# Constant 64-column products in TensorE's planned idle time of the first passes, and a new table of order shifts

## The chip, the cores and the metric

The kernel runs on one core of one Trainium2 chip. The metric is device time in microseconds (us), the median of several executions. Beside each kernel stands one profiled execution, whose span (first to last instruction) and own time are given with it. A difference of less than 0.3% is about what a measurement of this kernel can't tell from none.

## The reference

Attention with a block-causal mask, then two feed-forward layers, all in fp32:

```python
# q, k, v: (4, 8, 576, 64); w_in: (512, 2048), w_out: (2048, 512), twice
scores = q @ k.T / 8;  mask: key block (64 wide) <= query block
x = softmax(scores) @ v                      # -> 2304 tokens x 512
h = x @ w_in;  x = (h * tanh(softplus(h))) @ w_out       # layer 0
h = max(x @ w_in2, 0);  out = (h * h) @ w_out2           # layer 1
```

## The kernel before

The 2304 tokens are cut into six chunks of 384 tokens (CH1). Chunks 0 and 1 hold the first 192 tokens of two batches each (attention_lo, fp32 products), chunks 2 to 5 the last 384 tokens of one batch each (attention_hi, products of fp16 pairs). Each chunk goes through layer 0 and layer 1, so there are twelve passes over it (PASSES); a pass has 16 blocks f, each of which makes 12 products of 384 columns into a bank hp (line 1129), an activation on ScalarE (1135), and 12 products into the four banks acc (1195). Pass 0 is done in fp32 instead (lines 1149 and 1164). The weights arrive as words that VectorE and ScalarE first turn into fp32 (decode, lines 992 to 998) and then into fp16 pairs (split, lines 1008 to 1016 and parts, 966 to 967 and 678); the pairs go to DRAM and come back for later passes. This decoding, the attention of chunks 0 to 3 and the first passes share the first 230 us.

Nothing in the order of the program is left to a run-time scheduler. The class Sched (line 161) holds a list of tasks with an engine, a cost and dependencies each; forward (336) simulates the engines, takes at each step the ready task with the lowest rank, and gives it a start; the instructions are then issued in the order of those starts (1412 to 1417), on every engine and on the DMA queue (SP). The rank is a due time less a lead, and the lead takes a hand-held number of ns from the table SHIFT for each group of tasks: the attention of a chunk (att, av), the decoding of a weight unit (decode, weigh, split), the scaling of a chunk (scale, norm). A change of SHIFT so changes the order on all engines.

Sched.clock (227) models TensorE's clock: work counts at half speed in a stretch of time that follows a stretch with little work. Sched.fill (239) counts how many constant products (ones times ones, 128 columns, bf16) fit ahead of a TensorE task into the time in which TensorE is planned idle, and half of them are issued there (line 1416). It is called only while the pair of banks called spare is still free, that is until the first task of the rings ab and s1 on TensorE; afterwards no such products are issued.

spare is one tile of two PSUM banks of 512 fp32 columns. Columns 0 to 447 of both hold attention scores and their products: the ring ab takes both banks at once (attention_hi), the ring s1 alternately the one and the other (attention_lo). Columns 448 to 511 of bank 0 hold results of one to eight columns: sc (split, line 1009), qm (scale_of, 741), vm (halves, 693), sx (chunk_scale, 1070). Columns 448 to 511 of bank 1 are used by nothing. The planner holds these column ranges for separate resources. The waits between engines are put in by the framework when the program is built, from what each instruction reads and writes.

Of the kernel before, what the change touches and what calls it, by code (L numbers as in the profile page):

```python
# [56 lines left out]
def seg_len(tiles):  # L57
# [25 lines left out]


SHIFT = {
    ('att', 0, 0): 2800, ('att', 0, 1): 5100, ('att', 0, 2): -400, ('att', 0, 3): -4900,
    ('att', 0, 4): -400, ('att', 0, 5): 200, ('att', 0, 6): -800, ('att', 0, 7): -19200,
    ('att', 1, 0): 18800, ('att', 1, 1): 20600, ('att', 1, 2): 6300, ('att', 1, 3): -900,
    ('att', 1, 4): 29600, ('att', 1, 5): -29900, ('att', 1, 6): -33600, ('att', 1, 7): -28200,
    ('att', 2, 0): 200, ('att', 2, 1): -500, ('att', 2, 2): -900, ('att', 2, 3): 1000,  # L90
    ('att', 3, 0): -600, ('att', 3, 1): -500, ('att', 3, 2): 15300, ('att', 3, 3): 12900,
    ('att', 4, 0): -5700, ('att', 4, 1): 16600, ('att', 4, 2): 63500, ('att', 4, 3): 46400,
    ('att', 5, 0): -41600, ('att', 5, 1): 37300, ('att', 5, 2): 6700, ('att', 5, 3): 71800,
# [8 lines left out]
    ('decode', 0, 0, 0): -12000, ('decode', 0, 0, 1): 500, ('decode', 0, 0, 2): -22800, ('decode', 0, 0, 3): 21300,  # L102
    ('decode', 0, 0, 4): -19000, ('decode', 0, 0, 5): 5800, ('decode', 0, 1, 0): 21900, ('decode', 0, 1, 2): 119000,
    ('decode', 0, 1, 3): -17400, ('decode', 0, 1, 4): -11600, ('decode', 0, 1, 5): 100, ('decode', 0, 1, 6): 2900,
    ('decode', 1, 0, 0): -2900, ('decode', 1, 0, 1): -5700, ('decode', 1, 0, 2): 2500, ('decode', 1, 0, 3): 6300,
    ('decode', 1, 0, 4): 6800, ('decode', 1, 0, 5): 300, ('decode', 1, 0, 6): -600, ('decode', 1, 0, 7): -500,
    ('decode', 1, 1, 0): 1200, ('decode', 1, 1, 1): -14800, ('decode', 1, 1, 2): 17100, ('decode', 1, 1, 3): -20100,
    ('decode', 1, 1, 4): -1200, ('decode', 1, 1, 5): -5000, ('decode', 1, 1, 6): -14700, ('decode', 1, 1, 7): 50100,
    ('norm', 0, 1): -4700, ('norm', 0, 2): 4300, ('norm', 0, 3): -33900, ('norm', 0, 4): -90800,
    ('norm', 0, 5): -34000, ('norm', 1, 0): -2000, ('norm', 1, 1): -2000, ('norm', 1, 2): -21300,  # L110
    ('norm', 1, 3): 600, ('norm', 1, 4): -28700, ('norm', 1, 5): -2900, ('scale', 0, 1): -1800,
    ('scale', 0, 2): -2500, ('scale', 0, 3): 16300, ('scale', 0, 4): -43900, ('scale', 0, 5): 10000,
    ('scale', 1, 0): -8900, ('scale', 1, 1): 4000, ('scale', 1, 2): -46700, ('scale', 1, 3): 7800,
    ('scale', 1, 4): -15300, ('scale', 1, 5): -39200, ('split', 0, 0, 0): 100, ('split', 0, 0, 1): -3400,
    ('split', 0, 0, 2): -38000, ('split', 0, 0, 3): -39500, ('split', 0, 0, 4): 27000, ('split', 0, 0, 5): 9400,
    ('split', 0, 0, 6): -26000, ('split', 0, 0, 7): -26900, ('split', 0, 1, 0): -15000, ('split', 0, 1, 1): 800,
    ('split', 0, 1, 2): 46900, ('split', 0, 1, 3): -16600, ('split', 0, 1, 4): 98700, ('split', 0, 1, 5): -6500,
    ('split', 0, 1, 6): 1000, ('split', 0, 1, 7): -700, ('split', 1, 0, 0): 59200, ('split', 1, 0, 1): -5500,
    ('split', 1, 0, 2): 11900, ('split', 1, 0, 3): 2400, ('split', 1, 0, 4): 31500, ('split', 1, 0, 5): -59600,
    ('split', 1, 0, 6): 800, ('split', 1, 0, 7): -21100, ('split', 1, 1, 0): -1100, ('split', 1, 1, 1): -21300,  # L120
    ('split', 1, 1, 2): 24200, ('split', 1, 1, 3): -2700, ('split', 1, 1, 4): 5600, ('split', 1, 1, 5): -5300,
    ('split', 1, 1, 6): -78300, ('split', 1, 1, 7): 16600, ('weigh', 0, 0, 0): -67400, ('weigh', 0, 0, 1): -29800,
    ('weigh', 0, 0, 2): -31000, ('weigh', 0, 0, 3): -10000, ('weigh', 0, 0, 4): 1400, ('weigh', 0, 0, 5): 17000,
    ('weigh', 0, 0, 6): 35100, ('weigh', 0, 0, 7): 43100, ('weigh', 0, 1, 0): -33900, ('weigh', 0, 1, 1): -44700,
    ('weigh', 0, 1, 2): -12700, ('weigh', 0, 1, 3): -25600, ('weigh', 0, 1, 4): -5500, ('weigh', 0, 1, 5): 11700,
    ('weigh', 0, 1, 6): 42200, ('weigh', 0, 1, 7): 13700, ('weigh', 1, 0, 0): 14000, ('weigh', 1, 0, 1): -1500,
    ('weigh', 1, 0, 2): -100, ('weigh', 1, 0, 3): 1000, ('weigh', 1, 0, 5): -4400, ('weigh', 1, 0, 6): 4600,
    ('weigh', 1, 0, 7): 10900, ('weigh', 1, 1, 0): 4100, ('weigh', 1, 1, 1): 1400, ('weigh', 1, 1, 2): 1500,
    ('weigh', 1, 1, 4): -2600, ('weigh', 1, 1, 5): 2700, ('weigh', 1, 1, 6): -6400, ('weigh', 1, 1, 7): 193000,
}  # L130


# [28 lines left out]
class Sched:  # L161
# [4 lines left out]
    URGE = 20000.0  # L166
    TICK, DUTY = 10240.0 / 3, 0.375
    PHASE = 700.0
    SPARE = {}
    FIRST = {"PE": 300.0, "ACT": 1300.0, "DVE": 700.0}  # L170
    FILL, GUARD = 0.0, 300.0
    ROUNDS = 2
    SHARE = 0.5

# [61 lines left out]
            now += step  # L236
        t.dur = now - start

    def fill(self, now, start, t, where):

        n = 0
        while True:
            f = Task()
            f.dur, f.rows = self.FILL, 1.0
            busy = dict(self.busy)
            self.clock(f, now)
            if now + f.dur > start - self.GUARD:
                self.busy = busy
                break
            now += f.dur  # L250
            n += 1
        t.fillers = int(n * self.SHARE), where

    def build(self, order):
        for ring in self.rings:
# [78 lines left out]
        return sorted(self.tasks, key=lambda t: (t.start, t.idx))  # L334

    def forward(self):
        engs, self.busy, self.spare = {}, {}, dict(self.SPARE)
        for t in self.tasks:
            t.eng, t.dur, t.fn, t.lock = t.opts[0] if t.opts else t.first
            t.fillers = None  # L340
# [35 lines left out]
        while len(done) < len(self.tasks):  # L376
            best = None
            for name, (free, wait, ready) in engs.items():
# [36 lines left out]
            start = now  # L415
# [14 lines left out]
            elif name == "POOL":  # L430
                start = max(start, port[0])
            elif name == "DVE" and t.lock:
                start = max(start, port[1])
            if name == "PE":
                if t.final:
                    self.spare[t.final] = False
                place_ = [k for k, free in self.spare.items() if free]
                if place_ and self.FILL:
                    self.fill(e[0], start, t, place_[0])
            t.start = start  # L440
            if name == "PE":
                self.clock(t, start)
            end = start + t.dur
# [6 lines left out]
            if name == "SP":  # L450
                if t.xpose:
                    end = max(end, xpose + 170.0)
# [45 lines left out]
def tile_attention_moe(ctx, tc, qk, qp, va, vd, w1, w2, out):  # L498
    nc = tc.nc
# [4 lines left out]
    sch = Sched()  # L504
# [25 lines left out]
    def fixed(tiles):  # L530
        return sch.ring(len(tiles), lambda i: tiles[i % len(tiles)])
# [4 lines left out]
    R = {}  # L536
# [39 lines left out]
    att = ctx.enter_context(ExitStack())  # L576
# [41 lines left out]
    R["hp"] = fixed(hps)  # L618

    spare = {"ab": psp.tile([128, 2, 512], F32, tag="pab", name="spare")}  # L620
    sch.SPARE = {k: True for k in spare}

    R["sc"] = fixed([spare["ab"][:, 0, 448 + 4 * i:452 + 4 * i] for i in range(4)])
    R["qm"] = fixed([spare["ab"][:, 0, 464:472], spare["ab"][:, 0, 472:480]])
    R["sx"] = fixed([spare["ab"][:, 0, 496:504], spare["ab"][:, 0, 504:512]])
# [6 lines left out]
    ones = cp.tile([128, 128], BF16, name="ones")  # L632
# [634 lines left out]
    n = NX  # L1267
# [138 lines left out]
                t.deps.update(zeros)  # L1406

    follow(R["ab"].insts[0:1], R["s1"].insts)
    for inst in R["ab"].insts + R["s1"].insts:
        for t in inst.tasks:  # L1410
            t.final = "ab" if t.eng == "PE" else None
    seq = sch.run(order)
    with tc.manual_schedule():
        for t in seq:
            for _ in range(t.fillers[0] if t.fillers else 0):
                nc.tensor.matmul(out=spare[t.fillers[1]][:, 1, 0:128], lhsT=ones, rhs=ones, start=True, stop=True)
            t.fn()
    return sch


Sched.FILL=53.5
Sched.GUARD=100.0
Sched.SLACK=2.585517759996262
Sched.SHY={}
CH1=[[(0,LO),(1,LO)],[(2,LO),(3,LO)],[(2,HI)],[(0,HI)],[(3,HI)],[(1,HI)]]
# [87 lines left out]
```

## Time and profile before

| | us |
|---|---|
| median of 3 runs (lowest, highest) | 956.32 (954.38, 957.67) |
| the profiled execution: its time | 958.3 |
| the profiled execution: its span | 956.5 |
| of it TensorE busy | 913.7 |
| ScalarE busy | 612.3 |
| VectorE busy | 591.1 |

In the views below PE is TensorE, PEld its weight loads, DVE VectorE, ACT ScalarE, POOL GpSimd, SP the DMA queue's engine; L12 is line 12 of the kernel. An instruction's operands are written out<-in by the names of the program's tiles. PEclk is the clock that was granted to TensorE, as a share of 2.4 GHz; 0.50 is 1.2 GHz. "idle before <-" names what ended the idle time ahead of an instruction. Busy times of pipelined products overlap, and a busy engine isn't always at its peak.

### The profile page before, as it was taken

How to read it: one execution, taken by the hardware profiler on the slowest of the kernel's cores; microseconds unless marked ns; L12 is line 12 of the kernel's file. 1: busy time of each engine (PE TensorE's matmuls, PEld its weight loads, DVE VectorE, ACT ScalarE, POOL GpSimd, SP SyncE). 2: the span in 40 equal slices, each digit the busy share in tenths (PEclk: the TensorE clock that was granted, in tenths of full speed). 3: DMA queues.
4: the chain of work that ended last, by engine and by line, in shares of the span. 5: the costliest groups of instructions: out<-in, count | busy, mean ns of one | idle time of the engine just before them, and what ended most of it. 6: DMA issues, size and time to landing. Idle time of an engine off the chain costs nothing. (4 is left out here: it accounts for less than half of the span.)

```text
span 956.5 us, 15734 instructions
## 1 busy us (share of the span) xinstructions
PE 913.7 (96%) x5730; PEld 539.4 (56%) x5730; DVE 591.1 (62%) x1468; ACT 612.3 (64%) x1157; POOL 101.3 (11%) x129
## 2 busy tenths in 40 slices
PE   8888999699999899999999999999999999999997
PEld 7455455355655456555566555555566666666664
DVE  6788889988899997365661297687551241331211
ACT  6698789898779886465873376676742342443442
POOL 0000010322122121011010021121000000010000
PEclk9699999799999999999999999999999999999999
DMA  9677447789767989594772278697742112333430
GB/s 346 232 249 275 145 118 222 164 211 234 271 239 234 306 248 225 181 244 137 177 198 66 91 189 200 178 245 163 191 117 76 63 65 75 106 127 143 166 110 34
DMA packets 141774, 168.81 MB, mean 176 GB/s; under 512 B 105856, under 2 KB 110976, under 8 KB 137600
## 3 DMA queue, kind: packets, MB, share of 16 engines
q1 hardware_dynamic: 141696, 167.80, 60.2%
q8 instruction: 45, 0.74, 0.3%
q14 instruction: 33, 0.27, 0.1%
HBM read 125.30 MB, written 17.30 MB: 149 GB/s over the span
## 5 line engine op out<-in xcount | busy, mean ns | idle before, releaser
L678 DVE SCALAR_TENSOR_TENSOR g<-h,cst,g 128x384 f16<-128x384 f32 x176 | 110.8, 632 | 251.2 <-ACT g L966 237.4
L1135 ACT ACTIVATE h<-hp,cst 128x384 f32<-128x384 f32 x176 | 101.4, 578 | 220.7 <-PE hp L1129 220.2
L1195 PE MATMUL acc<-g,ws 128*128 128x384 f16 x1128 | 234.3, 326 | 0.0
L1195 PE MATMUL acc<-g,raw 128*128 128x384 f16 x984 | 207.9, 326 | 0.0
L1129 PE MATMUL hp<-x,first 128*128 128x384 f16 x768 | 162.9, 331 | 1.7 <-ACT h L1135 1.7
L1195 PEld LDWEIGHTS <-ws 128*128 128x128 f16 x1128 | 109.2, 98 | 73.6 <-issue 2.0
L1195 PEld LDWEIGHTS <-raw 128*128 128x128 f16 x984 | 95.5, 98 | 65.3 <-issue 2.6
L1129 PEld LDWEIGHTS <-first 128*128 128x128 f16 x960 | 92.7, 99 | 67.9 <-issue 9.7
L1129 PE MATMUL hp<-x,raw 128*128 128x384 f16 x552 | 118.8, 326 | 0.0
L967 POOL TENSOR_SCALAR g<-h,cst 128x384 f16<-128x384 f32 x64 | 56.1, 877 | 331.5 <-PE acc L1195 89.0
L1129 PE MATMUL hp<-x,ws 128*128 128x384 f16 x408 | 87.2, 332 | 0.3 <-DMA ws<-wspill 0.3
L1129 PEld LDWEIGHTS <-raw 128*128 128x128 f16 x648 | 61.2, 98 | 43.3 <-issue 4.1
L678 DVE SCALAR_TENSOR_TENSOR pb<-pad,st,pb 128x384 f16<-128x384 f32 (+2 forms) x96 | 72.6, 768 | 10.4 <-ACT pb L800 10.0
L782 ACT ACTIVATE pad<-spare,st,sq 128x448 f32<-128x448 f32 (+1 forms) x96 | 65.4, 682 | 20.4 <-DVE st L777 8.8
L800 ACT ACTIVATE pb<-pad,st 128x384 f16<-128x384 f32 (+2 forms) x96 | 65.3, 713 | 13.8 <-DMA pt<-pb 6.0
L966 ACT ACTIVATE g<-h,cst 128x384 f16<-128x384 f32 x112 | 68.6, 614 | 5.7 <-PE acc L1195 3.8
L1129 PEld LDWEIGHTS <-ws 128*128 128x128 f16 x504 | 48.6, 99 | 37.0 <-issue 5.1
L1149 PE MATMUL hp<-xs,first 128*128 128x384 f32 x128 | 55.6, 528 | 0.0
L774 DVE TENSOR_REDUCE st<-spare 128x2 f32<-128x896 f32 (+1 forms) x48 | 47.7, 993 | 5.2 <-PE spare L766 4.7
L1140 ACT ACTIVATE h<-h 128x384 f32<-128x384 f32 x87 | 44.5, 512 | 0.8
L766 PE MATMUL spare<-q 64*128 64x448 f16 (+2 forms) x384 | 38.9, 309 | 4.6 <-ACT pad L782 4.4
L1129 PE MATMUL hp<-late,first 128*128 128x384 f16 x192 | 41.7, 326 | 0.0
(221 smaller groups left out, 1165.8 us busy)
## 6 DMA issues: line engine op xcount, KB each, us to landing
ws<-wspill SPq DMA_DIRECT2D x68, 512.0 KB, 4.4
raw<-wspill SPq DMA_DIRECT2D x68, 512.0 KB, 4.0
raw<-in_w_dram SPq DMA_DIRECT2D x27, 1024.0 KB, 6.0
wspill<-wn SPq DMA_DIRECT2D x24, 512.0 KB, 4.9
qk<-in_qp_dram SPq DMA_DIRECT2D x16, 480.0 KB, 4.2
pad<-in_w_dram SPq DMA_DIRECT2D x5, 1024.0 KB, 6.1
vs<-in_va_dram SPq DMA_DIRECT2D x16, 320.0 KB, 3.4
out_dram<-ev SPq DMA_DIRECT2D x24, 192.0 KB, 2.5
```

Of the source, the lines that this page charges most:

```text
L678: return sch.add("DVE", c_dve(n) + 62 * ap, lambda: nc.vector.scalar_tensor_tensor(dst(), a(), s() if ap else s, c(), op0, op1), r=r, w=w, ...
L766: nc.tensor.matmul(out=pp.t[:, hd, o:o + k1 - k0], lhsT=qh.t[rows, u, a:a + 128], rhs=qh.t[rows, w, nq + k0:nq + k1], start=p == 0, stop=p ...
L774: sch.add("DVE", c_dve(2 * (o1 - o0)), lambda: nc.vector.reduce_max(both(st, j, r0), pp.t[r0:, :, o0:o1], axis=AX.X), w=[(pp, 0), (st, j)])
L782: sch.add("ACT", c_act(o1 - o0, True, 3), lambda hd=hd: nc.scalar.activation(pf[hd].t[r0:, k0:k0 + o1 - o0], pp.t[r0:, hd, o0:o1], AF.Exp, ...
L800: sch.add("ACT", c_act(n, False, 1), lambda pb=pb, pv=pv, s=s: nc.scalar.activation(pb.t[:, 0:i + 1, 0, :], pv(), AF.Copy, scale=s()), r=[ ...
L966: "ACT": ("ACT", c_act(n, False, 1), lambda: nc.scalar.activation(dst(0), src(), AF.Copy, scale=s()), False),
L967: "POOL": ("POOL", c_pool(n, False), lambda: nc.gpsimd.tensor_scalar(dst(0), src(), s(), 1.0, ALU.mult, ALU.mult), False),
L1129: nc.tensor.matmul(out=hp.t[:, 0:n], lhsT=w.t[:, f % 2, a, 128 * k:128 * k + 128], rhs=x.t[:, c, k, 0:n], start=k == 0 and i == 0, stop=k ...
L1135: sch.add("ACT", c_act(n, True, 1), lambda: nc.scalar.activation(h.t[:, 0:n], hp.t[:, 0:n], (AF.Mish, AF.Relu)[l], scale=hs()), r=[(cst, ( ...
L1140: "ACT": ("ACT", c_act(n), lambda: nc.scalar.activation(hv(), hv(), AF.Square), False),
L1149: nc.tensor.matmul(out=hp.t[:, 0:n], lhsT=wf.t[:, 512 * (f % 2) + 128 * k:512 * (f % 2) + 128 * k + 128], rhs=xs.t[:, k, 0:n], start=k == ...
L1195: nc.tensor.matmul(out=acc.t[:, 0:n], lhsT=wo.t[:, f % 2, a, 128 * m:128 * m + 128], rhs=g.t[:, c, 0:n], start=f == 0 and i == 0, stop=f = ...
```

## The change

Sched.fill is now called for each TensorE task whose planned start lies before 230 us (FEND), wherever TensorE is planned idle. It fills 0.6 of the idle time less 100 ns (SHARE, GUARD), with products priced at 45 ns in the plan (FILL) that count for 0.6 of their time as work for the modelled clock (FROWS). The planned start of the task behind them can't be earlier than their end. The products are now 64 columns wide and write columns 448 to 511 of bank 1 of spare. They are issued on TensorE directly ahead of their task, in the same order of starts as everything else; the planner gives them no dependencies. All the rest of the kernel's instructions stay, but nearly all numbers of SHIFT are new, so the order of the attention, decoding, splitting and scaling groups is another on all engines and on the DMA queue.

```diff
-    ('att', 0, 0): 2800, ('att', 0, 1): 5100, ('att', 0, 2): -400, ('att', 0, 3): -4900,
+    ('att', 0, 0): -9800, ('att', 0, 1): 1200, ('att', 0, 2): -8600, ('att', 0, 3): -8000,
...
-    FILL, GUARD = 0.0, 300.0
+    FILL, GUARD, FROWS, FEND = 0.0, 300.0, 0.6, 230000.0
...
-    def fill(self, now, start, t, where):
-
-        n = 0
-        while True:
-            f = Task()
-            f.dur, f.rows = self.FILL, 1.0
-            busy = dict(self.busy)
+    def fill(self, now, start, t):
+
+        n, end = 0, now + self.SHARE * (start - self.GUARD - now)
+        f = Task()
+        while now < end:
+            f.dur, f.rows = self.FILL, self.FROWS
             self.clock(f, now)
-            if now + f.dur > start - self.GUARD:
-                self.busy = busy
-                break
             now += f.dur
             n += 1
-        t.fillers = int(n * self.SHARE), where
+        t.fillers = n
+        return now
...
-                if t.final:
-                    self.spare[t.final] = False
-                place_ = [k for k, free in self.spare.items() if free]
-                if place_ and self.FILL:
-                    self.fill(e[0], start, t, place_[0])
+                t.fillers = 0
+                if self.FILL and start < self.FEND:
+                    start = max(start, self.fill(max(e[0], self.FIRST["PE"]), start, t))
...
-            for _ in range(t.fillers[0] if t.fillers else 0):
-                nc.tensor.matmul(out=spare[t.fillers[1]][:, 1, 0:128], lhsT=ones, rhs=ones, start=True, stop=True)
+            for _ in range(t.fillers or 0):
+                nc.tensor.matmul(out=spare["ab"][:, 1, 448:512], lhsT=ones, rhs=ones[:, 0:64], start=True, stop=True)
...
-Sched.FILL=53.5
+Sched.FILL=45.0
 Sched.GUARD=100.0
+Sched.SHARE=0.6
```

## Rows read from the trace of the kernel before

**Rows 1.** The page's head: busy time and share, and the granted clock in 40 slices.
```profile
span 956.5 us, 15734 instructions
PE 913.7 (96%) x5730; PEld 539.4 (56%) x5730; DVE 591.1 (62%) x1468; ACT 612.3 (64%) x1157; POOL 101.3 (11%) x129
PEclk9699999799999999999999999999999999999999
```

**Rows 2.** Stages: stretch, its length, busy us of each engine, clock, DMA share, GB/s.
```profile
10.00:140.00 130.00, 116.30 (x501) 69.96 (x500) 109.19 (x325) 105.67 (x227) 6.03 (x7) 0.91 0.67 230
140.00:200.00 60.00, 49.42 (x277) 27.39 (x276) 57.40 (x123) 56.17 (x90) 10.55 (x12) 0.91 0.68 172
200.00:230.00 30.00, 29.11 (x203) 16.93 (x204) 24.76 (x56) 28.95 (x46) 8.44 (x8) 1.00 1.09 265
230.00:956.50 726.50, 711.47 (x4729) 418.02 (x4723) 396.24 (x951) 418.03 (x787) 75.23 (x93) 1.00 0.57 162
```

**Rows 3.** The same view: stretches between 10 and 230 us at clock 0.50.
```profile
27.50:39.00 11.50, 9.50 (x33) 5.59 (x32) 8.40 (x24) 10.52 (x23) 0.00 (x0) 0.50 0.96 348
39.00:44.60 5.60, 4.88 (x15) 2.64 (x14) 2.88 (x7) 1.30 (x2) 0.00 (x0) 0.50 0.00 1
82.10:85.50 3.40, 3.40 (x13) 2.26 (x12) 1.64 (x4) 3.40 (x7) 0.00 (x0) 0.50 0.85 348
119.70:123.10 3.40, 3.37 (x7) 1.86 (x7) 3.34 (x12) 2.15 (x4) 2.77 (x4) 0.50 0.38 149
170.90:174.30 3.40, 3.03 (x10) 1.43 (x10) 3.38 (x13) 3.38 (x4) 0.00 (x0) 0.50 1.07 188
177.70:184.50 6.80, 5.29 (x20) 2.37 (x21) 6.75 (x19) 6.27 (x10) 4.12 (x6) 0.50 0.41 139
```

**Rows 4.** The same view: stretches ahead of four falls of the clock.
```profile
24.00:27.50 3.50, 2.04 (x16) 1.24 (x16) 3.03 (x11) 3.32 (x8) 0.00 (x0) 1.00 0.98 378
79.00:82.10 3.10, 1.91 (x14) 1.46 (x15) 3.10 (x8) 3.07 (x6) 0.00 (x0) 1.00 0.74 227
116.00:119.70 3.70, 1.92 (x14) 0.80 (x14) 2.54 (x19) 3.04 (x7) 0.00 (x0) 1.00 1.00 421
167.00:170.90 3.90, 1.66 (x17) 0.84 (x16) 3.58 (x7) 3.90 (x7) 0.00 (x0) 1.00 0.55 86
```

**Rows 5.** TensorE's waits, 10 to 230 us: total us, times, longest us.
```profile
PE spare L693 <- DVE sv L691: 3.6, 1, 3.6
PE spare L766 <- ACT pad L782: 3.3, 3, 1.6
PE spare L922 <- ACT pt L909: 2.4, 2, 1.8
PE hp L1091 <- ACT nsq L1086: 1.7, 1, 1.7
PE spare L741 <- ACT pt L909: 1.5, 1, 1.5
PE spare L1009 <- ACT pt L654: 1.3, 2, 0.7
...
PE spare L899 <- ACT pt L654: 1.1, 1, 1.1
```

**Rows 6.** ScalarE, then TensorE, in order of time: start, us, instruction [idle before <-releaser].
```profile
33.25 0.19 ACT L1008 ACTIVATION_READ_ACCUMULATOR wsq<-late 128x1 f32 x1
33.34 0.53 ACT L654 ACTIVATE pt<-spare 128x448 f32<-128x448 f32 x1
33.92 0.16 PE L1009 MATMUL spare<-us,onesq 128*128 128x1 bf16 x1 [0.69 <-ACT pt L654]
```

**Rows 7.** TensorE in order of time: constant products of before, and two one-column products.
```profile
1.05 1.35 PE L1416 MATMUL spare<-ones 128*128 128x128 bf16 x11 [1.05 <-DVE ones L633]
163.86 0.19 PE L1009 MATMUL spare<-us,onesq 128*128 128x1 bf16 x2 [1.24 <-DVE xm L1174]
```

**Rows 8.** ScalarE in order of time: a wait for TensorE.
```profile
44.88 0.49 ACT L1154 ACTIVATE h<-hp 128x384 f32<-128x384 f32 x1 [4.56 <-PE hp L1149]
```

More of the change, by code (lines that the diff above doesn't have):

```diff
@@ L85 @@
 SHIFT = {
-    ('att', 0, 0): 2800, ('att', 0, 1): 5100, ('att', 0, 2): -400, ('att', 0, 3): -4900,
[L87 to L91, printed above, removed]
@@ L92 @@
-    ('att', 4, 0): -5700, ('att', 4, 1): 16600, ('att', 4, 2): 63500, ('att', 4, 3): 46400,
-    ('att', 5, 0): -41600, ('att', 5, 1): 37300, ('att', 5, 2): 6700, ('att', 5, 3): 71800,
[8 rows of a table removed]
-    ('decode', 0, 0, 0): -12000, ('decode', 0, 0, 1): 500, ('decode', 0, 0, 2): -22800, ('decode', 0, 0, 3): 21300,
-    ('decode', 0, 0, 4): -19000, ('decode', 0, 0, 5): 5800, ('decode', 0, 1, 0): 21900, ('decode', 0, 1, 2): 119000,
-    ('decode', 0, 1, 3): -17400, ('decode', 0, 1, 4): -11600, ('decode', 0, 1, 5): 100, ('decode', 0, 1, 6): 2900,
@@ L105 @@
[L105 to L129, printed above, removed]
+    ('att', 0, 0): -9800, ('att', 0, 1): 1200, ('att', 0, 2): -8600, ('att', 0, 3): -8000,
@@ new lines @@
+    ('att', 0, 4): 19000, ('att', 0, 5): -2800, ('att', 0, 6): 44300, ('att', 0, 7): -15900,
+    ('att', 1, 0): -13900, ('att', 1, 1): 28600, ('att', 1, 2): 28600, ('att', 1, 3): 2800,
+    ('att', 1, 4): 39600, ('att', 1, 5): -44000, ('att', 1, 6): -8400, ('att', 1, 7): -7700,
+    ('att', 2, 0): 200, ('att', 2, 1): -500, ('att', 2, 3): 1700, ('att', 3, 0): 4700,
+    ('att', 3, 1): -500, ('att', 3, 2): 13800, ('att', 3, 3): -7400, ('att', 4, 0): -17800,
+    ('att', 4, 1): 25600, ('att', 4, 2): 73700, ('att', 4, 3): 45200, ('att', 5, 0): -20400,
@@ new lines @@
+    ('att', 5, 1): 45300, ('att', 5, 2): 5100, ('att', 5, 3): 25900, ('av', 0, 0): -12500,
[8 rows of a table added]
+    ('decode', 0, 0, 2): 4000, ('decode', 0, 0, 3): 19000, ('decode', 0, 0, 4): -28200, ('decode', 0, 0, 5): 400,
+    ('decode', 0, 0, 6): -600, ('decode', 0, 0, 7): -800, ('decode', 0, 1, 0): 46200, ('decode', 0, 1, 1): 68300,
+    ('decode', 0, 1, 2): 126400, ('decode', 0, 1, 3): -33400, ('decode', 0, 1, 4): -33900, ('decode', 0, 1, 5): -500,
+    ('decode', 0, 1, 6): 2200, ('decode', 0, 1, 7): -400, ('decode', 1, 0, 0): 40300, ('decode', 1, 0, 1): -11100,
@@ new lines @@
+    ('decode', 1, 0, 2): 2000, ('decode', 1, 0, 3): 19000, ('decode', 1, 0, 4): 6800, ('decode', 1, 0, 5): 1200,
+    ('decode', 1, 0, 6): -11100, ('decode', 1, 0, 7): 400, ('decode', 1, 1, 0): -39400, ('decode', 1, 1, 1): -15600,
+    ('decode', 1, 1, 2): 16600, ('decode', 1, 1, 3): -20300, ('decode', 1, 1, 4): -1000, ('decode', 1, 1, 5): -6900,
+    ('decode', 1, 1, 6): -13900, ('decode', 1, 1, 7): -1000, ('norm', 0, 1): -5500, ('norm', 0, 2): 20700,
+    ('norm', 0, 3): -34300, ('norm', 0, 4): -87900, ('norm', 0, 5): -30600, ('norm', 1, 0): 12700,
@@ new lines @@
+    ('norm', 1, 1): -3700, ('norm', 1, 2): -19700, ('norm', 1, 3): 34800, ('norm', 1, 4): -17500,
+    ('norm', 1, 5): -28100, ('scale', 0, 1): -10900, ('scale', 0, 2): 11000, ('scale', 0, 3): 14800,
+    ('scale', 0, 4): -31800, ('scale', 0, 5): -52300, ('scale', 1, 0): -21800, ('scale', 1, 1): -400,
+    ('scale', 1, 2): 22000, ('scale', 1, 3): -28400, ('scale', 1, 4): -14300, ('scale', 1, 5): -57300,
+    ('split', 0, 0, 0): -5100, ('split', 0, 0, 1): -77700, ('split', 0, 0, 2): -48300, ('split', 0, 0, 3): -40000,
@@ new lines @@
+    ('split', 0, 0, 4): 29900, ('split', 0, 0, 5): 11300, ('split', 0, 0, 6): -2700, ('split', 0, 0, 7): -200,
+    ('split', 0, 1, 0): -44000, ('split', 0, 1, 1): -8800, ('split', 0, 1, 2): 72300, ('split', 0, 1, 3): -11900,
+    ('split', 0, 1, 4): 99700, ('split', 0, 1, 5): -8100, ('split', 0, 1, 6): -1300, ('split', 0, 1, 7): 1100,
+    ('split', 1, 0, 0): 54100, ('split', 1, 0, 1): 19300, ('split', 1, 0, 2): -9200, ('split', 1, 0, 3): -400,
+    ('split', 1, 0, 4): 2900, ('split', 1, 0, 5): -54400, ('split', 1, 0, 6): 21900, ('split', 1, 0, 7): -24300,
@@ new lines @@
+    ('split', 1, 1, 0): 23500, ('split', 1, 1, 1): -18600, ('split', 1, 1, 2): 68800, ('split', 1, 1, 3): -4700,
+    ('split', 1, 1, 4): 12500, ('split', 1, 1, 5): 13700, ('split', 1, 1, 6): -37500, ('split', 1, 1, 7): -28600,
+    ('weigh', 0, 0, 0): -66800, ('weigh', 0, 0, 1): -29100, ('weigh', 0, 0, 2): -31100, ('weigh', 0, 0, 3): -8900,
+    ('weigh', 0, 0, 4): 3200, ('weigh', 0, 0, 5): 13000, ('weigh', 0, 0, 6): 20600, ('weigh', 0, 0, 7): 43900,
+    ('weigh', 0, 1, 0): -43800, ('weigh', 0, 1, 1): -55200, ('weigh', 0, 1, 2): -12600, ('weigh', 0, 1, 3): -33300,
@@ new lines @@
+    ('weigh', 0, 1, 4): 6200, ('weigh', 0, 1, 5): -22500, ('weigh', 0, 1, 6): -6400, ('weigh', 0, 1, 7): -5000,
+    ('weigh', 1, 0, 0): 13600, ('weigh', 1, 0, 1): 8900, ('weigh', 1, 0, 2): -300, ('weigh', 1, 0, 3): 2800,
+    ('weigh', 1, 0, 5): -4300, ('weigh', 1, 0, 6): 51100, ('weigh', 1, 0, 7): 2900, ('weigh', 1, 1, 0): 6700,
+    ('weigh', 1, 1, 1): 1200, ('weigh', 1, 1, 2): 13200, ('weigh', 1, 1, 4): -12300, ('weigh', 1, 1, 5): -33300,
+    ('weigh', 1, 1, 6): -6500, ('weigh', 1, 1, 7): 206600,
@@ L168 @@
     PHASE = 700.0
-    SPARE = {}
     FIRST = {"PE": 300.0, "ACT": 1300.0, "DVE": 700.0}
-    FILL, GUARD = 0.0, 300.0
+    FILL, GUARD, FROWS, FEND = 0.0, 300.0, 0.6, 230000.0
     ROUNDS = 2
@@ L336, in forward @@
     def forward(self):
-        engs, self.busy, self.spare = {}, {}, dict(self.SPARE)
+        engs, self.busy = {}, {}
         for t in self.tasks:
@@ L620, in tile_attention_moe @@
     spare = {"ab": psp.tile([128, 2, 512], F32, tag="pab", name="spare")}
-    sch.SPARE = {k: True for k in spare}
     R["sc"] = fixed([spare["ab"][:, 0, 448 + 4 * i:452 + 4 * i] for i in range(4)])
@@ L1408, in tile_attention_moe @@
     follow(R["ab"].insts[0:1], R["s1"].insts)
-    for inst in R["ab"].insts + R["s1"].insts:
-        for t in inst.tasks:
-            t.final = "ab" if t.eng == "PE" else None
     seq = sch.run(order)
```

16 rows, old and new, of the table SHIFT are left out of this document.

## The prediction

> **What bounds the kernel now.** I read the page's head first: TensorE is busy for 96% of the span, and the granted clock is well under full in two slices, both among the first eight [rows 1]. The busy time by stage then splits the run [rows 2]. From 230 us to the end TensorE is busy 711.47 of 726.50 us at clock 1.00: that part is bound by products which the change neither adds nor removes. From 10 to 230 us TensorE is busy 194.8 of 220 us (116.30 + 49.42 + 29.11), so 25.2 us are idle, and two of the three stages stand at clock 0.91. There VectorE and ScalarE are the other candidates: from 140 to 200 us they are busy 57.40 and 56.17 of 60, so that stage is theirs, not TensorE's; from 10 to 140 us they have 16% and 19% left.
>
> The clock is at 0.50, that is at 1.2 GHz, in six stretches of 34.1 us together [rows 3]. Before four of the falls TensorE had been busy only about half of the time: 2.04 of 3.50, 1.91 of 3.10, 1.92 of 3.70 and 1.66 of 3.90 us [rows 4]. The list of TensorE's waits says where the idle time comes from: long waits for ScalarE and VectorE in the attention of chunks 1 to 3 [rows 5].
>
> **The change: the clock.** The products are meant to keep TensorE active in those waits, so that the clock doesn't fall. In the six stretches TensorE is busy 29.5 us; the same products at 2.4 GHz need half, so at most 14.7 us can come back [rows 3]. Much of that is no gain. From 27.5 to 39 us ScalarE is busy 10.52 of 11.50, and after 170.9 us VectorE is busy 10.13 of 10.20: faster products only wait longer there. From 39.0 to 44.6 us neither is busy (2.88 and 1.30 of 5.60), so half of 4.88, 2.4 us, is gained. In the stretches at 82.1 and 119.7 us TensorE has no idle time (3.40 and 3.37 of 3.40), but one of the others is saturated too; I count them as gains, 1.7 us each, because TensorE has a backlog there. Sum 5.8 us; the ends are 14.7 gained and, if a clock that the new order disturbs elsewhere falls once more, 1.7 lost.
>
> **The change: the new order.** Of the waits, those of up to 1.8 us for L922, 1.5 for L741 and 1.1 for L899 lie before 140 us where the other engines have room; I take these 4.4 us as gone [rows 2, 5]. The rest I leave, since from 140 to 200 us no order can make VectorE shorter. The best end is all 25.2 us. The worst is that the new order waits everywhere as before it does from 140 to 200 us: 10.58 us idle in 60 [rows 2], so 38.8 in 220, which is 13.6 more. DMA issues move with the order, since SP follows the same starts: from 200 to 230 us the DMA share is already 1.09 [rows 2], but no wait of TensorE's for a DMA is among those of rows 5, and I count nothing. After 230 us I leave the 15.0 us of idle time as they are; a third more or less would be 5.0 us.
>
> **The change: the products themselves.** The idle time of 25.2 us times 0.6 is 15.1 us of constant products, about 335 at the plan's 45 ns. For their pace the trace has bounds: eleven 128-column ones took 1.35 us at the start, ends included, some 107 ns each at the low clock, and the second of two one-column products ends only 0.03 us after the first would have (0.19 against 0.16 us) [rows 6, 7]. So 64 columns lie between 30 and 54 ns, and 45 is kept. Each brings a weight load, which overlaps. They use no DMA and no other engine. By the Trainium skill (TensorE: Matmul & The Clock Gate, "Wait — 56ns, not 53.3ns?") a product takes its columns over 2.4 GHz plus some 2.5 ns, an estimate of 29 ns for 64 columns; the term below would then be 1.9 instead of 2.9 us. No row here shows 64 columns of bf16 at the high clock.
>
> In a true gap they cost nothing, since TensorE waits anyway. The question is whether they can run in it. At 33.25 us ScalarE reads the sum that the one-column product L1009 uses, done by 33.44; L1009 starts at 33.92, when ScalarE's L654, which reads columns 0 to 447 of spare, is done at 33.87 [rows 6]. L1009 writes other columns, from 448 on, and uses nothing of L654's. So a write to the unused columns of a score bank waits for readers of the scores. The new products write such columns, in bank 1. If a gap is a wait for a reader of that bank, they start when it ends, and the real product stands behind them. The waits of rows 5 whose releaser uses spare (L782, L909, L654: 3.3 + 2.4 + 1.5 + 1.3 + 1.1) are 9.6 us; times 0.6 that is 5.8 us of products that run late. attention_lo alternates the banks, so I take half of it, 2.9 us, and 0 and 15.1 (all of them late) as ends.
>
> **The sum.** -5.8 - 4.4 + 2.9 = -7.3 us. The profiled execution took 958.3 us, so 951.0; the median of the runs is 2.0 us under it, so 949.0 us. Its own range is 944 to 953.
>
> **Rivals.**
> - *The products lock the score bank (slower).* All 15.1 us of them run after their gaps. On top of that a reader of bank 1 that is issued behind some of them waits until TensorE, in its order, has come past them, so ScalarE's exponentials hang on TensorE's backlog; the one long wait of ScalarE for TensorE in the trace is 4.56 us [rows 8], and one such is counted. With 5.8 + 4.4 us still gained: 956.3 - 10.2 + 15.1 + 4.6 = 965.8. Without that wait it decides from 10.2 us of late products, two thirds of them. For it: L1009's wait [rows 6]. Against: 3.6 us behind L693 and 1.7 behind L1091 [rows 5] are waits for vs and nsq, which have nothing to do with spare. The Trainium skill (PSUM — Partial Sum Buffer, "PSUM bank collisions raise a hardware error") says the same as a rule: engines are to be kept apart by bank and group of 32 partitions, not by address. The trace agrees, with the 0.48 us between L1008's end and L1009's start.
> - *VectorE and ScalarE bound it (no change).* Between 10 and 200 us they are busy 167 and 162 of 190 us [rows 2]; a TensorE that is faster or better fed then only waits elsewhere. Only the 2.4 us at 39 us come back, and late products take 1 of them: 955.
> - *The order gains much more.* Idle time from 10 to 200 us is 24.3 us [rows 2]; if half goes, 12.2, with 5.8 of clock and 2.9 of late products: 941.2. For it: nearly all shifts are new, and the plan need no longer keep TensorE dense for the clock. Against: rows 2 from 140 to 200 us.
> - *The products don't hold the clock and the order is a worse one.* The 34.1 us at 0.50 stay somewhere, and idle time grows by the 13.6 us above with nothing gained: 969.9.
>
> **How the numbers follow.** Forecast 0.35, locked bank 0.22, no change 0.20, order gains more 0.16, worse order 0.07. What a measurement can tell is 0.3%, 2.9 us: faster is the forecast (0.34 of it) and the large order gain, 0.50; within is the no-change case and small parts of the forecast and of the locked bank, 0.23; slower the rest of the locked bank and the worse order, 0.27. The range reaches down to 939 (0.07 left out below) and up to 966 (0.12 above): the large order gain less 3 us, and the locked bank.
>
> **What would show it.** Right: the six stretches of rows 3 are gone or short, with clock 1.00 from 10 to 230 us; the constant products begin as soon as the task ahead of them ends, and stand inside idle stretches; the task behind them starts within 0.2 us of its releaser; the passes after 230 us begin some 7 us earlier than before. Wrong by the locked bank: groups of constant products whose first has an idle time ended by L782, L909, L654 or L774, and ScalarE or VectorE instructions on spare released by a constant product. Wrong by the others: VectorE and ScalarE idle as little as before while TensorE's idle time stays; or clock 0.50 in other stretches. Most easily wrong is the order, since one table of shifts moves every engine and the trace of before says nothing of the new one.

## The result, and the profile after

| | us |
|---|---|
| kernel before, median of 6 runs (lowest, highest) | 955.78 (954.38, 957.98) |
| changed kernel, median of 6 runs (lowest, highest) | 961.61 (959.99, 963.11) |
| ratio, 95% interval | 1.0057 (1.0039 to 1.0074) |
| changed kernel, profiled execution: time, span | 962.2, 960.4 |

The changed kernel is slower by 0.6%, twice what a measurement can tell from nothing. The time lies in the range that was given only because that reached up to 966 us for the rival of the locked bank; the direction was forecast wrong.

The page's head and the stages of the changed kernel (columns as in [rows 1, 2]):

```profile
span 960.4 us, 16306 instructions
PE 914.7 (95%) x6012; PEld 544.5 (57%) x6012; DVE 590.7 (62%) x1467; ACT 621.0 (65%) x1165; POOL 99.9 (10%) x130
```

```profile
10.00:140.00 130.00, 116.47 (x564) 71.58 (x563) 110.91 (x322) 105.60 (x227) 4.94 (x7) 0.95 0.66 232
140.00:200.00 60.00, 46.23 (x435) 29.71 (x434) 50.51 (x117) 54.94 (x88) 8.55 (x9) 0.91 0.54 143
200.00:230.00 30.00, 29.57 (x209) 17.36 (x209) 26.06 (x53) 28.06 (x42) 5.79 (x7) 1.00 0.86 245
230.00:960.40 730.40, 715.26 (x4763) 418.82 (x4760) 399.65 (x963) 428.81 (x801) 79.55 (x98) 1.00 0.57 164
```

The clock rose, as intended: 0.95 where it was 0.91 from 10 to 140 us. With the two levels 1.2 and 2.4 GHz a mean of 0.95 over 130 us is 13.0 us at the low level and 0.91 over 60 us is 10.8, together 23.8 us where [rows 2] give 34.2. But from 140 to 200 us TensorE is busy 46.23 us where it was 49.42, though 10.37 us of that, by the same view of line 1406, are now constant products; VectorE, which was saturated there, has 9.5 us idle; and ScalarE's busy time over the whole span grew from 612.3 to 621.0 us, for which eight more table loads of 1.28 us each are enough. After 230 us the idle time is 15.1 us, as before (15.0).

TensorE's waits from 10 to 230 us (line 1406 is the constant products; total us, times, longest):

```profile
PE spare L1406 <- ACT pad L775: 9.9, 4, 5.3
PE spare L1406 <- ACT pt L902: 3.0, 2, 1.7
```

These rows stand where those of [rows 5] stood: the engine still waits for ScalarE's exponentials (L775 is L782 of before, L902 is L909), but now it is the constant products that wait. After 10 us 275 of them run, and 227 stand in nine groups that wait between 0.76 and 5.33 us and run, 10.5 us in all by their rows, when the wait has ended. The largest of these places, on TensorE and then ScalarE, in order of time:

```profile
188.66 4.01 PE L1406 MATMUL spare<-ones 128*128 128x64 bf16 x76 [5.33 <-ACT pad L775]
192.60 0.74 PE L759 MATMUL spare<-q 64*128 64x448 f16 x6
```

```profile
188.70:192.00 3.30, 3.30 (x64) 3.30 (x64) 2.25 (x5) 1.80 (x2) 0.00 (x0) 0.50 1.00 262
```

```profile
188.41 0.19 ACT L775 ACTIVATION_READ_ACCUMULATOR pad<-spare,st,sq 128x1 f32 x1
...
193.38 0.61 ACT L745 ACTIVATE q<-qk,sq 128x384 f16<-128x384 f32 x1 [2.87 <-PE spare L759]
```

TensorE is idle for 5.33 us until the last reader of the scores is done at 188.60. Then 76 constant products run, from 188.66 until the scores start at 192.60, nearly all of them at clock 0.50, to which it had fallen in the idle time that they were to fill. Only then come the scores L759, which could have started at 188.66 themselves, and ScalarE waits 2.87 us for them. Elsewhere ScalarE's exponentials wait for the constant products themselves, L902 for 0.69 us at 28.53 and for 1.32 us at 31.89. The products that were to fill a gap have become its continuation.

### The profile page after: what moved, and what is told of

It is laid out like the page before. It is cut to its first block, busy times and chain, and to the rows that moved or that the text cites. A ratio compares the mean times of both kernels' runs of the same rounds, so it can differ in the third digit from the quotient of the medians.

```text
span 960.4 us, 16306 instructions
## 1 busy us (share of the span) xinstructions
PE 914.7 (95%) x6012; PEld 544.5 (57%) x6012; DVE 590.7 (62%) x1467; ACT 621.0 (65%) x1165; POOL 99.9 (10%) x130
## 5 line engine op out<-in xcount | busy, mean ns | idle before, releaser
L1122 PE MATMUL hp<-x,first 128*128 128x384 f16 x768 | 160.3, 327 | 0.4 <-ACT h L1128 0.4
L960 POOL TENSOR_SCALAR g<-h,cst 128x384 f16<-128x384 f32 x61 | 51.4, 844 | 305.4 <-PE acc L1188 62.5
L775 ACT ACTIVATE pad<-spare,st,sq 128x448 f32<-128x448 f32 (+1 forms) x96 | 65.4, 682 | 18.0 <-DVE tl L814 6.4
L959 ACT ACTIVATE g<-h,cst 128x384 f16<-128x384 f32 x115 | 70.6, 614 | 9.7 <-DVE cst L1111 5.2
L1142 PE MATMUL hp<-xs,first 128*128 128x384 f32 x128 | 52.8, 503 | 0.0
L1133 ACT ACTIVATE h<-h 128x384 f32<-128x384 f32 x83 | 42.2, 511 | 0.5
L1157 PE MATMUL acc<-h,late 128*128 128x384 f32 x96 | 41.4, 524 | 0.0
```

The lines of the kernel that those rows point to most:

```text
L775: sch.add("ACT", c_act(o1 - o0, True, 3), lambda hd=hd: nc.scalar.activation(pf[hd].t[r0:, k0:k0 + o1 - o0], pp.t[r0:, hd, o0:o1], AF.Exp, ...
L959: "ACT": ("ACT", c_act(n, False, 1), lambda: nc.scalar.activation(dst(0), src(), AF.Copy, scale=s()), False),
L960: "POOL": ("POOL", c_pool(n, False), lambda: nc.gpsimd.tensor_scalar(dst(0), src(), s(), 1.0, ALU.mult, ALU.mult), False),
L1122: nc.tensor.matmul(out=hp.t[:, 0:n], lhsT=w.t[:, f % 2, a, 128 * k:128 * k + 128], rhs=x.t[:, c, k, 0:n], start=k == 0 and i == 0, stop=k ...
L1133: "ACT": ("ACT", c_act(n), lambda: nc.scalar.activation(hv(), hv(), AF.Square), False),
L1142: nc.tensor.matmul(out=hp.t[:, 0:n], lhsT=wf.t[:, 512 * (f % 2) + 128 * k:512 * (f % 2) + 128 * k + 128], rhs=xs.t[:, k, 0:n], start=k == ...
```

## The experiments

The ratios are to the kernel before on the same chip. Line numbers shift by a few between the kernels. Three edits recur. "None" takes away the constant products, except at the start. "Spare" is the products of the change, in bank 1 of spare. "Free" puts them, from the first sums of pass 0 on, into the accumulator bank acc3, which no engine reads until a pass ends. While a sum is open there they add zeros to it (nil is a tile of zeros); between two sums they write its unused columns. The lines that keep note of opened and closed sums are left out here:

```diff
-                nc.tensor.matmul(out=spare["ab"][:, 1, 448:512], lhsT=ones, rhs=ones[:, 0:64], start=True, stop=True)
+                if opened.get(3):
+                    nc.tensor.matmul(out=opened[3].t[:, 0:64], lhsT=ones, rhs=nil, start=False, stop=False)
+                else:
+                    bank = closed[3].t if 3 in closed else spare["ab"][:, 1]
+                    nc.tensor.matmul(out=bank[:, 448:512], lhsT=ones, rhs=ones[:, 0:64], start=True, stop=True)
```

For the old order the counts are worked out after the planning, so that the rest of the program keeps its order:

```diff
     seq = sch.run(order)
+    free = Sched.FIRST["PE"]
+    late = {}
+    for t in seq:
+        if t.eng == "PE":
+            if 10000.0 < t.start < 230000.0:
+                late[t] = max(0, int(0.6 * (t.start - 100.0 - free) / 45.0 + 0.999))
+            free = t.start + t.dur
```

| constant products | old order | new order |
|---|---|---|
| none | 1 (the kernel before) | 1.0032 (1.0017 to 1.0046) |
| bank 1 of spare | 1.0052 (1.0033 to 1.0071) | 1.0057 (1.0039 to 1.0074) |
| free, in acc3 | 0.9986 (0.9971 to 1.0000) | 1.0030 (1.0011 to 1.0050) |

**The new order without the products (new_none).**

```diff
-            for _ in range(t.fillers or 0):
+            for _ in range((t.fillers or 0) if t.start < 10000.0 else 0):
```

> The changed kernel's order, with the constant products after the first 10 us of the plan left out (the 18 at the start stay). Theory 1 (the products lock the score bank): the nine groups that wait for readers of the scores and then run ahead of a real product take some 10 us in the changed kernel; without them 951 to 957 us. Theory 2 (the new order is the worse one): 961 us as with them, or up to 966 us, since the clock then falls more often. Theory 3 (both about even): 957 to 960 us.

Measured 960.3 us, 1.0032, between theories 2 and 3. Some 0.3% of the loss is the order's own (with the plan that made it), and the products add about 0.25%, 0.23 either way. The stages of this kernel, and two of TensorE's waits in it:

```profile
10.00:140.00 130.00, 118.18 (x510) 71.69 (x510) 110.17 (x322) 104.97 (x227) 4.96 (x7) 0.92 0.66 231
140.00:200.00 60.00, 47.56 (x262) 25.51 (x261) 54.07 (x125) 58.99 (x95) 9.87 (x9) 0.86 0.60 152
200.00:230.00 30.00, 29.66 (x196) 16.98 (x198) 25.51 (x50) 28.08 (x45) 4.87 (x6) 1.00 0.93 266
```

```profile
87.62 0.16 PE L734 MATMUL spare<-sq,ones 128*128 128x2 bf16 x1 [1.84 <-ACT pt L902]
187.80 1.30 PE L759 MATMUL spare<-q 64*128 64x448 f16 x6 [4.88 <-ACT pad L775]
```

TensorE's idle time from 10 to 230 us is 24.6 us, against 25.2 of before: the new order took nothing of it away, it moved it. Up to 140 us TensorE gains 1.9 us of busy time; from 140 to 200 us it loses as much, and there ScalarE is now busy 58.99 of 60 us. The low clock takes 37.6 us where it took 34.2. The two traces are only 1.0 us apart in span (957.5 and 956.5), so they show where time goes, but not all of the 0.32%.

**The products alone on the old order (old_spare).**

> The old order, instruction for instruction, with 64-column constant products into bank 1 of spare added in 0.6 of each planned idle time of TensorE between 10 and 230 us (some 170 of them). Theory 1: they wait and run late, 170 times 30 to 53 ns is 5 to 9 us less what later gaps and the clock give back: 957 to 963 us. Theory 2: 952 to 956 us, the products themselves do no harm.

Measured 962.4 us, 1.0052, as theory 1 had it: the 184 new products alone cost half a percent. A place of this trace, VectorE, TensorE and ScalarE in order of time:

```profile
178.38 0.15 DVE L1015 TENSOR_SCALAR wst<-spare 128x2 uint32<-128x2 uint32 x1
178.59 2.53 PE L1425 MATMUL spare<-ones 128*128 128x64 bf16 x44 [2.31 <-DVE wst L1015]
181.19 0.62 ACT L782 ACTIVATE pad<-spare,st,sq 128x320 f32<-128x320 f32 x1 [2.99 <-PE spare L693]
```

L1015 reads sc, which lies in bank 0; the products write bank 1 and wait for it all the same, 2.31 us. Behind them stands L693, and ScalarE's exponentials wait 2.99 us for that. So the lock isn't a bank's but that of the whole tile spare, both banks. The trace of the kernel before bears this out: of its 483 instructions of VectorE and ScalarE on spare none overlaps a TensorE product into spare, though the ring s1 alternates the banks; on the two banks hp, which are two tiles, 147 of 225 do.

**The same into an open sum of acc3 (new_acc, old_acc).** Here the products went to acc3 only while a sum was open there, and else to spare.

> The changed kernel's order and number of constant products, but while a sum is open in the accumulator bank acc3 they add zeros to it (64 columns, zero moving operand) instead of writing bank 1 of spare, so they wait for no reader of the scores. Theory 1: they run inside the gaps, the waits of the constant products for ScalarE's L775 and L902 are gone, the clock stays at 1.00 in more of the 23.9 us that are at 0.50 in the changed kernel: 949 to 955 us. Theory 2: no better than without them, 960 to 964 us.

> The old order with the same constant products as zeros into the open sum of acc3. Theory 1: 951 to 955 us, with clock 1.00 in most of the six stretches that were at 0.50. Theory 2: 953 to 957 us. If the clock falls in the same stretches as before, zero products of 64 columns don't hold it, and this run tells nothing of the lock.

Measured 1.0071 (1.0047 to 1.0095) and 1.0035 (1.0011 to 1.0059). Neither is better than the same order without products (1.0032 and 1): theory 1 missed in both, and old_acc lies above theory 2 too. The traces say why: from 155 to 192 us, between the sums of pass 0 and pass 1, no sum is open, so the products there went to spare as before and waited as before. In the old order only two groups of six went to acc3 at all. The first row is of old_spare, the others are of old_acc, TensorE in order of time:

```profile
84.50 0.34 PE L1425 MATMUL spare<-ones 128*128 128x64 bf16 x6 [1.05 <-ACT pt L654]
```

```profile
78.72 0.33 PE L1433 MATMUL acc<-nil,ones 128*128 128x64 bf16 x6
79.92 1.09 PE L902 MATMUL spare<-vs 128*128 128x192 f32 x6 [0.86 <-ACT pt L657]
```

It is the second of these groups, ahead of the same scores. In spare it waits 1.05 us for ScalarE's copy; in acc3 it starts at once, and the wait of 0.86 us that is left stands behind it.

**The products without the lock everywhere (new_free, old_free).**

> The changed kernel with its 293 constant products, but from the first sums of pass 0 on they write the accumulator bank acc3 (zeros added to its open sum, or its unused columns between two sums) and not bank 1 of spare. Theory 1 (the lock is what the products cost): the groups behind 150 us start when the task ahead of them ends, their waits for L775 are gone, some 8 us of late products go: 953 to 957 us. Theory 2 (the new order is the worse one, the lock adds the rest): about the changed order without products, 958 to 961 us. If it stays at 961 to 964 us, the products' cost isn't the lock.

> The old order with the 195 constant products, from pass 0 on in acc3 in the same way. Theory 1: below the kernel before, 951 to 955 us, since pass 0 already ended 4 us earlier with some of them in acc3 and those at 160 to 190 us no longer run late. Theory 2 (VectorE and ScalarE bound the stage from 140 to 200 us): 955 to 958 us, what is won in pass 0 is waited away there.

Measured 960.7 us, 1.0030, as theory 2 had it, and 955.6 us, 0.9986, at the border of the two theories. The group of 76 in new_free (line 1419 is the products, 762 the scores), and the stages of old_free:

```profile
180.60 2.39 PE L1419 MATMUL acc<-ones 128*128 128x64 bf16 x76
188.00 1.30 PE L762 MATMUL spare<-q 64*128 64x448 f16 x6 [5.02 <-ACT pad L778]
```

```profile
188.00:189.30 1.30, 1.30 (x7) 0.36 (x7) 1.30 (x4) 1.29 (x2) 0.00 (x0) 0.50 1.03 218
```

```profile
10.00:140.00 130.00, 113.85 (x562) 69.81 (x561) 110.87 (x326) 107.34 (x228) 6.01 (x7) 0.96 0.66 231
140.00:200.00 60.00, 51.83 (x419) 30.85 (x419) 57.94 (x125) 57.09 (x90) 12.10 (x13) 0.97 0.69 179
...
230.00:955.30 725.30, 709.11 (x4708) 416.43 (x4705) 393.95 (x948) 415.74 (x783) 74.52 (x93) 1.00 0.57 162
```

The lock is what the products cost: without it they run at the start of their gap, and the scores wait for ScalarE alone. In either order the difference between spare and free is a loss: 0.66% in the old one, 6.3 us (0.24% either way), and 0.27% in the new one, 2.6 us (0.26% either way, so at the edge of what can be told). But the gain that the products were added for is small. In old_free the low clock is down from 34.2 to 14.0 us (0.04 of 130 and 0.03 of 60, doubled), and the time falls by 0.14%, 1.4 us, at the edge of its interval. At 230 us TensorE has 2.4 us more of its work behind it (709.11 busy us left for 711.47), and of that 1.2 us come back as idle time later (16.2 for 15.0 us). In the new order the gain is nothing: the low clock is down from 37.6 to 20.2 us, at 230 us TensorE is only 0.6 us ahead of new_none, and after it the idle time is 17.7 us for 15.3. old_free is the best version seen that computes the same, but not by more than a measurement can tell.

**Without the one large group (no_76).**

```diff
-            for _ in range(t.fillers or 0):
+            for _ in range((t.fillers or 0) if (t.fillers or 0) < 60 else 0):
```

> The changed kernel without one group of its constant products: the 76 that at 188.66 us waited 5.33 us for ScalarE's L775 and then ran 3.94 us ahead of the scores L759. Theory 1 (the lock, and here this group first of all): 2 to 4 us less than the changed kernel, so 1.002 to 1.004 of the kernel before, like the order without products. Theory 2 (late products are absorbed by VectorE's work): no less than 1.005.

Measured 963.6 us, 1.0080 (1.0059 to 1.0101): theory 1 missed, and the bound of theory 2 holds. In its trace the scores start 4.3 us earlier, and the idle time after 230 us is 20.7 us instead of 15.1:

```profile
188.31 1.30 PE L759 MATMUL spare<-q 64*128 64x448 f16 x6 [5.34 <-ACT pad L775]
```

```profile
230.00:962.70 732.70, 711.99 (x4743) 417.93 (x4742) 397.12 (x958) 426.10 (x794) 81.96 (x98) 1.00 0.57 162
```

So what looks like 4 us on the path was given back behind 230 us, and more; on which engine isn't shown, so theory 2's reason, VectorE, is neither. The rows show the lock; what one group of it costs at the end can't be read from its place.

**Without table loads (new_relu, old_relu).** ScalarE loads its table of functions when it turns from the exponentials to layer 0's activation and back, 1.28 us each time: 50 times in the old order, 58 in the new. These two kernels put Relu in place of Mish, so they compute something else; of the two lines the changed words are shown.

```diff
-(AF.Mish, AF.Relu)[l]
+(AF.Relu, AF.Relu)[l]
...
-AF.Mish
+AF.Relu
```

> The new order without constant products, with Relu in place of Mish in layer 0 (this part of the computation is changed), so that ScalarE needs no table load but the first. It had 58 loads of 1.28 us, the old order 50. Theory 2a (the 8 more loads are what makes the new order slower): the difference to the old order with the same edit goes from +3 us to 0 +- 1.5 us. Theory 2b (it is the order of the rest): the new order stays 2 to 5 us slower.

> The old order with Relu in place of Mish in layer 0 (this part of the computation is changed): 49 loads of 1.28 us are gone from ScalarE. If ScalarE bounds the first 230 us, where most of the loads are, this is 5 to 20 us faster than the kernel before; if VectorE or TensorE does, within 3 us of it. Reference for the same edit in the new order.

Measured 0.9935 (0.9915 to 0.9956) and 0.9907 (0.9891 to 0.9924). The new order stays 0.28% behind (0.26% either way), where it was 0.32% behind with the loads: the eight more loads aren't the whole cause; whether they are a part of it can't be told. And 49 loads, 62.9 us of ScalarE, are worth 9 us, which is in the range that was expected if ScalarE bounds the first 230 us. Of all the work that was taken off in these runs it is the only one that paid.

**Less work for VectorE (old_dve, old_free_dve, old_free_pool).** Up to pass 1's first product into acc VectorE had had nearly the same work in all traces so far, which pointed to it as the bound. The first two kernels leave out the step that restores the sign of layer 0's weights (L996); the third moves the scaling of attention weights (L685) to GpSimd and computes the same.

```diff
-        sch.add("DVE", c_dve(n), lambda: nc.vector.scalar_tensor_tensor(
+        sch.add("DVE", c_dve(n), lambda: l == 1 and nc.vector.scalar_tensor_tensor(
             o(), words(1), 0x80000000, o(), ALU.bitwise_and, ALU.bitwise_or), r=[raw], w=[wf], lock=True)
```

> The old order with VectorE's L996, the step that restores the sign, left out in the 16 weight units of layer 0 (this part of the computation is left out): 16 times 1.14 us, 18.2 us less for VectorE, all before pass 1's first product into acc, up to which VectorE had 153 to 155 us of work in all eight runs. Theory 3 (VectorE sets the time of that product, and the end with it): 9 to 18 us faster, 939 to 948 us. If TensorE's idle time and low clock set it: 0 to 4 us faster.

> The old order with the lock-free constant products and without L996 in layer 0 (this part of the computation is left out). With VectorE relieved, TensorE's clock should count for more: theory 3 gives 3 to 6 us less than the same kernel without the products, where it was 1.4 us less with all of VectorE's work; if the held clock is worth nothing in any case, 0 to 2 us less.

> The old order with the lock-free constant products, and the scaling of the attention weights that stood on VectorE (L685, 7.2 us before 187 us) issued on GpSimd. Theory 3: 2 to 5 us less than with the products alone, 950 to 954 us, if GpSimd's longer operation (some 0.4 to 0.9 us for 0.3) doesn't delay the chain of chunk 0 and its memory traffic doesn't slow VectorE; otherwise up to 5 us more.

Measured 1.0018 (1.0001 to 1.0035), 0.9998 (0.9982 to 1.0014) and 1.0035 (1.0022 to 1.0048). The theory that VectorE's work ahead of pass 1 sets the end has fallen: with 14 us less of it before 140 us nothing is gained, though in the trace that first product comes 3.9 us earlier (183.65 for 187.59 us). TensorE's waits are those of before, as old_dve's from 10 to 200 us show, and so is VectorE's load from 140 to 200 us:

```profile
PE spare L693 <- DVE sv L691: 4.0, 1, 4.0
PE spare L766 <- ACT pad L782: 2.8, 2, 2.0
PE hp L1091 <- ACT nsq L1086: 2.7, 2, 1.7
PE spare L922 <- ACT pt L909: 2.6, 2, 2.0
```

```profile
140.00:200.00 60.00, 48.76 (x295) 27.12 (x294) 57.38 (x125) 56.72 (x91) 11.88 (x13) 0.91 0.73 192
```

The longest of these waits is for VectorE (L691), in the stage where it is busy 57.38 of 60 us as before. What VectorE's work there is worth none of these runs tells, as all of them take it off earlier. The held clock is worth 0.20% with VectorE relieved (0.23% either way) and 0.14% without, so no more is seen of it where VectorE has less to do before 140 us. Moving L685 to GpSimd made it worse, by 0.49% against old_free.

**The plan and the shifts apart (plan_old, plan_old_free, mix_early, mix_late).** All in the changed plan, with the table of shifts exchanged in whole or by halves; only plan_old_free has the constant products, without the lock.

> The changed plan with all old shifts, constant products at the start only. If the new shifts are the cause: 0.998 to 1.001 of the kernel before, since only the modelled clock differs. If the plan that counts on a held clock is the cause: 1.002 to 1.005.

> The changed plan with all old shifts and its constant products, from pass 0 on in acc3, where they wait for no reader of the scores. By what the old order gained from such products (0.9986): 0.15% less than the run without them, 0.996 to 1.000. If it beats the kernel before by more than 0.3%, the old shifts with a plan that holds the clock are the better version.

> The changed plan, constant products at the start only, with the new shifts for chunks 0 and 1, the weights of layer 0 and the scaling of layer 0 (90 of 180 keys) and the old ones for the rest. If the early half is what makes the new order slower: 1.002 to 1.005 of the kernel before. If it is the late half: 0.998 to 1.001. Two halves that were not chosen for each other can cost some more, up to 1.01, and that would then show in both mixes.

> The same with the old shifts for the early half and the new ones for the rest. If the early half is the cause: 0.998 to 1.001; if the late half: 1.002 to 1.005; up to 1.01 if halves of different tables don't fit together.

Measured 1.0277 (1.0245 to 1.0309), 1.0257 (1.0224 to 1.0290), 1.0185 (1.0144 to 1.0226) and 1.0166 (1.0133 to 1.0198). All four lie above the ranges that were expected. In the changed plan the new table makes 1.0032 (new_none) and the old one 1.0277, and a mix lies between them: the new early half takes 0.9% off, the new late half 1.1%. So both halves of the new table fit this plan better than the old ones. Which of them makes the new order slower than the old order in its own plan, as was asked, these runs can't say, and the new table in the old plan wasn't tried. The rows of plan_old show what the plan does with the old table, pass 1's first product into acc (it is at 187.59 us in the kernel before), then a stage:

```profile
170.97 0.66 PE L1187 MATMUL acc<-g,ws 128*128 128x384 f16 x3
```

```profile
230.00:400.00 170.00, 142.13 (x895) 79.02 (x894) 146.62 (x341) 130.66 (x216) 32.19 (x32) 0.90 0.79 233
```

Pass 1's first product comes 16.6 us earlier, and from 230 to 400 us TensorE then stands still for 27.9 us. The kernel before has this row for it, 6.6 us:

```profile
230.00:400.00 170.00, 163.37 (x1093) 95.00 (x1088) 142.21 (x333) 127.23 (x218) 31.10 (x32) 0.99 0.80 243
```

VectorE and ScalarE did much the same work in that stretch in both. TensorE's longest waits in plan_old from 230 to 400 us:

```profile
PE spare L1001 <- ACT wsq L1000: 4.4, 3, 2.4
PE spare L855 <- DVE wst L1007: 3.6, 1, 3.6
PE hp L1121 <- DMA ws<-wspill: 3.0, 1, 3.0
PE spare L1062 <- DVE xm L870: 2.5, 1, 2.5
```

They belong to the splitting of weights, the attention, weights on their way back from DRAM and the scaling. No single one of them makes up the 27.9 us; why they come together isn't shown.

## Why the prediction was wrong

*What bounds the kernel.* That from 140 to 200 us ScalarE and VectorE saturate was read rightly, and so was that TensorE's gaps there are waits for attention. What wasn't seen is that most of what is won on one engine in the first 230 us comes back as a wait later: 62.9 us off ScalarE gave 9 us, 14 us off VectorE before 140 us none, scores 4.3 us earlier on TensorE none. That ScalarE's is the only one that paid agrees with TensorE's waits, 16 of 25 us of which are for ScalarE in the kernel before.

*The clock, 5.8 us forecast.* The mechanism is right: products in the gaps keep the clock up (34.2 us at the low level, 23.8 in the changed kernel, 14.0 in old_free). The size is wrong: 1.4 us in the old order, none in the new one. In either order TensorE is ahead at 230 us by much less than the clock could give back (2.4 of 10.1 us and 0.6 of 8.7, half of what the low clock lost), as it waits more. The stretches at 82.1 and 119.7 us were counted as gains because TensorE was full there, although [rows 3] showed one of the others saturated in both. With those two left out the term would have been 2.4 us.

*The new order, 4.4 us forecast.* This is the step that failed. It is +0.32%, some 3 us, instead. Of the three waits that were taken as gone, that of L741 is still there, at L734, with 1.84 us; those of L922 and L899 fell to 0.8 and 0.5 us, but ahead of the last scores before pass 1 TensorE now waits 4.88 us where it waited 1.61. Idle time from 10 to 230 us is 24.6 us against 25.2, and the low clock took 3.4 us more. That a new table is another point on the same trade, and that no wait can be called gone before the new order is seen, would have put this term at zero with both ends wide. What in the new order costs the 3 us stays open. The lock of the products is ruled out, since new_none has none of them there; the clock too, since new_free holds it and is no faster; the table loads aren't all of it; and the halves of the table can't be told apart.

*The products, 2.9 us forecast.* The mechanism was read from one row of before [rows 6] and is shown: the waits of 9.9 and 3.0 us, the same group with and without a wait in old_spare and old_acc, and the difference of spare and free. The pace was bracketed rightly (30 to 54 ns forecast, 29 and 53 measured). The size at the end was less than half of the loss in the old order (6.3 us) and close to that in the new one (2.6 us), but that is in part luck: 10.5 us of products ran late, not 2.9, and a quarter of that shows at the end. Taking half of the waits because attention_lo alternates its banks was wrong, as the lock covers both banks. And 4.4 of the 9.6 us of waits behind this term are the same waits that the term of the order takes as gone.

*The rivals.* The locked bank came nearest, 965.8 us for 961.6. Its parts were as told: the groups wait for L775 and L902, 227 of 275 products are late, and ScalarE waits for a product behind them (2.87 us, where 4.6 were counted). Its point of decision, 10.2 us of late products, stood on gains of 10.2 us that weren't there; without them a few late microseconds decide. The case of no change had the truth about the clock.

## What to carry to other kernels

Filler work has to write where nobody reads: a write to unused columns waits for the readers of the rest of its tile, here of two banks, and filler that waits runs exactly when the engine is needed. A gap of an in-order engine is worth filling for the clock only if that engine sets the end afterwards; take the work off first and see whether the time moves. And a hand-tuned order is tuned to its plan: the old table in the changed plan cost 2.8% here, 26 us, where the whole change was forecast to gain 7.3.

## What the runs showed of the hardware

64-column bf16 products with a weight load each start 29 ns apart at the high clock (76 of them in 2.39 us in new_free, the last one's 0.19 us included) and 53 ns apart at the low one (188.7 to 192.2 us in the changed kernel; the last ones of that group, after the clock has risen, are 29 ns apart again). So the plan's 45 ns is too dear at the high clock and too cheap at the low one. By the Trainium skill (TensorE: Matmul & The Clock Gate, "Wait — 56ns, not 53.3ns?") a product takes its columns over 2.4 GHz plus some 2.5 ns when the clock is high, an estimate of 29 ns for 64 columns; the trace agrees. Because a group runs through so quickly and stands at the start of its gap, the clock can still fall before the gap ends: in new_free 5.02 us of idle time are left behind the 76, and the six scores after them run at clock 0.50 and take 1.30 us, where the same six take 0.74 in the changed kernel right behind its products.

A write to columns that nothing reads waited up to 5.33 us for readers of other columns of its bank, and 2.31 us for a reader of the other bank of its tile: these are waits that the framework puts into the program. The rule of the Trainium skill on PSUM (PSUM — Partial Sum Buffer, "PSUM bank collisions raise a hardware error") is to keep engines apart by bank and not by address. The first of the two waits agrees with it, and the second goes further than it asks.

Runs of one kernel scatter by more than what was sought: the kernel before gave 952.9 to 961.5 us in eleven runs of one comparison, so a single trace says where time goes but not how much 2 us of it are worth.
